# Window attention with a feed-forward block: the first batch's mask added by TensorE instead of VectorE

## The chip, the cores and the metric

One core of one Trainium2 chip runs the whole program. The metric is the device microseconds of an execution; runs are told by their median. The kernel before takes 974.76 us (median of 3 runs, 974.61 to 975.1).

The engines are named as the profile does: PE is TensorE's matmul, PEld its weight load, DVE VectorE, ACT ScalarE, POOL GpSimd, SP SyncE, which issues most of the DMAs here.

## The reference, cut to what matters

There are 8 batches of 8 heads, 512 local and 32 global rows in a head, 64 columns. A local row sees the 32 global keys and the local keys at most 32 places away. The attention's output, all heads of a row side by side, goes through a feed-forward block of 512 to 2048 to 512 columns.

```python
s_g = scale * np.matmul(q_g, k_all.transpose(0, 1, 3, 2))
out_g = np.matmul(sm(s_g), v_all)
s_ll = scale * np.matmul(q_l, k_l.transpose(0, 1, 3, 2))
mask = np.abs(pos[:, None] - pos[None, :]) <= window          # window = 32
s_ll = np.where(mask, s_ll, -1000000000.0)
s_l = np.concatenate([scale * np.matmul(q_l, k_g.transpose(0, 1, 3, 2)), s_ll], axis=-1)
out_l = np.matmul(sm(s_l), np.concatenate([v_g, v_l], axis=2))
...
h = x @ w_in
out = (h - np.tanh(h)) @ w_out
```

## The kernel before, in words

**The work and its tiles.** Heads are taken in pairs (class `Pair`), four pairs to a batch. In a pair, the keys and queries of two heads are loaded (`add_load`), turned on PE with an identity matrix `idr` (`add_turn`, L1046) and copied out of PSUM to `first_kw` and `first_q` (L869). A head has four tiles of 128 queries against 224 keys (`KC`). `scores` makes two tiles of both heads in one visit of PE (L1149), into one PSUM bank a head. `add_softmax` then works a head and a visit: `peak` (L1458) takes each tile's scores from PSUM, adds the tile's mask, scales by -0.125, writes the sum to a `prob` or `t` tile in SBUF and keeps the row's minimum in `st`, one instruction and one accumulator read a tile; `exp` (L1465) makes the exponentials in place on ACT, with their row sums. `add_norms` takes the inverse of the sums on DVE (L1221, L1222) and multiplies on POOL (L1228). `transposes` turns the probabilities on PE (L1170), copies bring them to `keys_first` (L869), and `add_product` multiplies them with the values (L1247) and splits the result in a high and a low part, `x_hi` (L869) and `x_lo` (L1258), for the feed-forward block. Global queries have their own path (L1079, L1080, L1084, L1090, L1097, L1117).

**The feed-forward block** of a batch (class `Chunk`) takes all heads of its 512 rows: hidden columns by L1520 (three passes, high and low parts of `x` and of `w_in`), tanh (L1528), difference (L1531) and its two parts, output by L1568. Its first step can't start before the last pair's `x_hi` is there. From then on, the feed-forward steps of one batch run on PE between the attention of the next. The weights arrive as 64-bit numbers and are joined to 32 bits on ACT and DVE (`rebias` L938, `low` L942, `join` L946), a piece at a time, then split in high and low parts (L869 and L952).

**Constants.** POOL writes the identity into `pg` (`identity`, masks.py:197 and :199) and the four bf16 masks (`mask(j)`, L1644 to L1650), DVE casts the identity to `idr` (L1636).

**The order.** Every step is an `Op` with engines, a duration and a due time; `Order.run` plans them on a model of the engines and writes each engine's instructions in the planned order. On the chip each engine works through its list strictly in that order. Due times come from `CFG` (some 100 numbers) plus `NUDGE`, a table from the place of an Op to a shift of its due time; `CHOICE` adds a cost to one engine of an Op that can go to two. Where the plan sees PE idle for 0.9 us or more between 5 and 72 us, it puts in filler matmuls of a mask with itself (`fill`, L1814) whose result nobody reads.

Of the kernel before, what the change touches and what calls it, by code (L numbers as in the profile page):

```python
# [10 lines left out]
BF16 = mybir.dt.bfloat16  # L11
# [5 lines left out]
P = 128  # L17
D = 64
# [186 lines left out]
def kernel(ctx, tc, q_l, k_l, v_l, q_g, k_g, v_g, w_in, w_out, out):  # L205
# [66 lines left out]
    masks = [cp.tile([P, KC], BF16, name=f"mask{j}") for j in range(NT)]  # L272
    stats = [cp.tile([P, 24], F32, name=f"st{j}") for j in range(2)]
# [19 lines left out]
    def bank(shape, j, dt=F32):  # L293
# [6 lines left out]
        elif len(shape) == 4:  # L300
# [7 lines left out]
               last=-56.3309, o_st0=-386.5366, o_st1=962.4127, o_tw0=-1908.8636, o_tw1=121.285, one=0, p0=167.5456, pen=5.1952,  # L308
               penp=47.4685, s_g=0.6459, s_gl=20.2886, s_kq=73.0039, s_p=1.9417, s_tg=0.5596, s_w=0.6068, s_wl=12.2887,
               step=102.1945, step1=21.2806, lag0=117.1894, hs0=56.6249, tol=0.0795, xs=0.0659, xw=9.5452, o_ld0=-439.2206,  # L310
               o_tn0=1501.0446, o_sg0=1021.2062, o_tg0=289.7609, o_s0=616.7985, o_sp0=196.7798, o_t0=745.3086, o_tpp0=876.351,
               o_vl0=1794.6857, o_vl1=734.9051, o_pv0=1974.7926, o_pvp0=642.1916, o_ld1=1133.7362, o_pv1=890.4116,
               o_pvp1=90.6808, o_s1=-787.3947, o_sg1=-1021.8773, o_sp1=285.1529, o_t1=-1317.1873, o_tg1=-727.1647,
               o_tn1=632.8924, o_tpp1=-8.455, ho0=190.6449, o_tg=2149.4869, o_pv=1266.5023, o_pvp=-608.8611, o_s=-973.7784,
               o_sp=-468.8434, o_t=-622.5358, o_tpp=348.926, o_tn=-382.6256, o_ld=423.028, o_lq=846.3999, o_sg=-1214.8469,
               o_st=-26.0002, o_tw=1592.5009, o_vl=-2037.6091, o_gl=-12.6939, a_kw=0.2609, d_kw=1.0519, s_kw=0.0614, wdi=0.6492,
               wdo=21.9692, L_a_g=0.8656, L_a_kg=6.9738, L_a_ph=2.8878, L_a_qs=197.4661, L_a_w=3.3975, L_a_wn=6.4235,
               L_a_xg=4.0116, L_d_g=0.6393, L_d_gl=0.5557, L_d_kg=0.1783, L_d_kq=1.1326, L_d_ph=1.8089, L_d_pl=8.7171,
               L_d_qh=0.7611, L_d_qs=907.9411, L_d_tg=8.6488, L_d_tp=8.6984, L_d_w=0.4061, L_d_wl=7.1153, L_d_wn=0.8306,
               L_d_xg=0.6352, L_d_y=0.615, L_ho=452.3556, L_hs=43.2601, L_lag=0.3314, L_last=0.1662, L_pen=0.2526, L_penp=1.0537,  # L320
               L_s_g=0.443, L_s_gl=4.8181, L_s_kq=0.3525, L_s_p=0.5472, L_s_tg=0.3595, L_s_w=1.024, L_s_wl=6.2232,
# [686 lines left out]
    class Pair:  # L1008
# [28 lines left out]
        def add_turn(self):  # L1037
# [18 lines left out]
            def queries(e, _):  # L1056
                copy(e, q, box[1])
# [573 lines left out]
    def add_constants():  # L1631
# [3 lines left out]
        def rounded(e, _):  # L1635
            nc.vector.tensor_copy(idr, pg[:, :P])  # L1636
# [214 lines left out]
```

## Time and profile before

| | |
|---|---|
| median of 3 runs | 974.76 us (974.61 to 975.1) |
| the profiled execution | 975.52 us, its span 973.7 us |
| PE busy in the span | 960.3 us (99%), 6453 matmul records |
| DVE, ACT, POOL busy | 580.3 us (60%), 452.1 us (46%), 387.3 us (40%) |
| the chain that ended last | PE 93%, DVE 2%, ACT 2%, SP 1%, DMA 1% |
| filler matmuls (L1814) | 93 |

Busy time of PE includes fillers, and matmuls that wait in its pipe. The chain names for each stretch the engine that the next step waited for, so the few per cent that aren't PE's show where PE itself is not the limit. A line in the rows below is that of kernel.py; L869 is the helper `copy`, used for many tiles. A record of an fp32 matmul comes twice in the trace, so a visit of `scores` with its four products shows as x8.

### The profile page before, as it was taken

What the parts mean: (1) busy time and instruction counts of PE and PEld (TensorE: products, weight loads), DVE (VectorE), ACT (ScalarE), POOL (GpSimd) and SP (SyncE); (2) the same over time, 40 slices, a digit from 0 to 9 for tenths busy, and PEclk for the clock granted to TensorE, in tenths of its full rate; (3) what the DMA queues carried; (4) which work ended last, traced back from release to release, by engine and by line L of the source; (5) the groups of instructions that cost most, each with busy time, mean ns of one, the idle gap of its engine ahead of it and who ended that gap; (6) DMA issues with size and microseconds to landing.
All of it is one profiled execution on the core that took longest, in us unless ns stands there. A gap on an engine that the chain in (4) does not pass through costs nothing.

```text
span 973.7 us, 18494 instructions
## 1 busy us (share of the span) xinstructions
PE 960.3 (99%) x6453; PEld 784.5 (81%) x6453; DVE 580.3 (60%) x1907; ACT 452.1 (46%) x1275; POOL 387.3 (40%) x526
## 2 busy tenths in 40 slices
PE   8899999999999999999999999999999999999998
PEld 5677877888888888888888888888888888888897
DVE  6997667766657555766676567657636544422211
ACT  6966575745455434654355444534535434111111
POOL 4666756534444433434234444333332332211221
PEclk9999999999999999999999999999999999999999
DMA  8565244321223121322123122221202200100010
GB/s 233 151 178 165 84 114 114 92 38 35 50 39 82 33 39 34 88 40 34 32 38 83 23 39 39 71 50 34 50 14 69 39 17 1 44 1 1 1 44 22
DMA packets 195166, 57.32 MB, mean 59 GB/s; under 512 B 179712, under 2 KB 188416, under 8 KB 195072
## 3 DMA queue, kind: packets, MB, share of 16 engines
q1 hardware_dynamic: 193728, 55.61, 24.1%
q8 instruction: 51, 0.84, 0.4%
q10 hardware_dynamic: 1344, 0.52, 0.2%
q14 instruction: 43, 0.35, 0.1%
HBM read 47.19 MB, written 8.91 MB: 58 GB/s over the span
## 4 chain that ended last, share of the span: by engine, by line
PE 93%; DVE 2%; ACT 2%; SPq 1%; issue 1%; DMA 1%; POOL 0%; POOLq 0%; DVEq 0%; ACTq 0%
PE bank L1520 39%; PE bank L1568 38%; PE bank L1247 6%; PE bank L1149 4%; PE bank L1170 4%; PE bank L1339 1%; SPq L1030 0%; PE bank L1046 0%; DMA wraw<-in_q_g_dram 0%; ACT t L1465 0%; ACT pg L1090 0%; POOL prob L1228 0%; DVE keys_first L869 0%; ACT prob L1465 0%; ACT keys_first L869 0%
## 5 line engine op out<-in xcount | busy, mean ns | idle before, releaser
L1537 POOL TENSOR_TENSOR glo<-t,ghi 128x512 fp32r<-128x512 f32 x107 | 139.1, 1301 | 328.9 <-PE bank L1568 130.0
L1528 ACT ACTIVATE t<-bank 128x512 f32<-128x512 f32 x136 | 81.3, 598 | 302.7 <-PE bank L1520 292.3
L1531 DVE TENSOR_TENSOR t<-bank,t 128x512 f32<-128x512 f32 x136 | 93.9, 691 | 202.5 <-ACT t L1528 201.8
L1228 POOL TENSOR_SCALAR prob<-prob,st 128x224 f32<-128x224 f32 x240 | 108.0, 468 | 143.3 <-DVE st L1222 124.9
L1568 PE MATMUL bank<-w_out_hi,ghi 128*128 128x512 f32 x544 | 152.7, 394 | 0.0
L1568 PE MATMUL bank<-w_out_hi,glo 128*128 128x512 f32 x544 | 151.5, 392 | 0.0
L1568 PE MATMUL bank<-w_out_lo,ghi 128*128 128x512 f32 x544 | 151.3, 392 | 0.0
L1520 PE MATMUL bank<-x_hi,w_in_hi 128*128 128x512 f32 x512 | 140.3, 397 | 0.3 <-DVE x_hi L869 0.3
L1520 PE MATMUL bank<-x_lo,w_in_hi 128*128 128x512 f32 x512 | 137.4, 390 | 0.0
L1520 PE MATMUL bank<-x_hi,w_in_lo 128*128 128x512 f32 x512 | 136.2, 390 | 0.0
L1465 ACT ACTIVATE prob<-prob,st 128x224 f32<-128x224 f32 x240 | 113.2, 475 | 14.9 <-DVE st L1458 13.7
L1458 DVE CUSTOM_DVE_ANT_0 prob<-bank,mask 128x224 f32<-128x224 f32 x240 | 80.8, 386 | 64.7 <-PE bank L1149 57.8
L1568 PEld LDWEIGHTS bank<-w_out_lo,ghi 128*128 128x128 f32 x544 | 101.1, 188 | 22.1 <-issue 1.0
L1568 PEld LDWEIGHTS bank<-w_out_hi,glo 128*128 128x128 f32 x544 | 101.0, 188 | 21.9 <-issue 0.7
L1568 PEld LDWEIGHTS bank<-w_out_hi,ghi 128*128 128x128 f32 x544 | 100.2, 188 | 22.2 <-issue 1.4
L1520 PEld LDWEIGHTS bank<-x_hi,w_in_hi 128*128 128x128 f32 x512 | 93.7, 188 | 24.7 <-issue 3.2
L1520 PEld LDWEIGHTS bank<-x_lo,w_in_hi 128*128 128x128 f32 x512 | 95.9, 188 | 20.2
L1520 PEld LDWEIGHTS bank<-x_hi,w_in_lo 128*128 128x128 f32 x512 | 95.7, 188 | 19.7
L869 ACT COPY keys_first<-bank 128x512 f32<-128x512 f32 (+2 forms) x150 | 69.9, 516 | 89.2 <-PE bank L1170 88.3
L1247 PE MATMUL bank<-keys_first,values 128*64 128x160 f32 (+3 forms) x1024 | 68.7, 276 | 2.2 <-DVE keys_first L869 1.1
L1247 PEld LDWEIGHTS bank<-keys_first,values 96*64 96x64 f32 (+1 forms) x1024 | 56.3, 136 | 9.5 <-ACT keys_first L869 2.9
L1381 DVE STREAM_TRANSPOSE gt<-pg 32x128 f32<-32x128 f32 x192 | 53.1, 276 | 10.2 <-POOL pg L1360 4.3
(164 smaller groups left out, 1222.9 us busy)
## 6 DMA issues: line engine op xcount, KB each, us to landing
values<-in_v_l_dram SPq DMA_DIRECT2D x128, 72.0 KB, 2.2
out_dram<-wpair SPq DMA_DIRECT2D x32, 256.0 KB, 2.0
rawkq<-in_k_l_dram SPq DMA_DIRECT2D x96, 64.0 KB, 2.3
rawkq<-in_q_l_dram SPq DMA_DIRECT2D x96, 64.0 KB, 2.2
values<-in_v_g_dram SPq DMA_DIRECT2D x64, 48.0 KB, 2.0
first_q<-in_moe_w_in_dram SPq DMA_DIRECT2D x6, 512.0 KB, 4.5
stage<-in_moe_w_out_dram SPq DMA_DIRECT2D x6, 512.0 KB, 4.0
stage<-in_moe_w_in_dram SPq DMA_DIRECT2D x6, 512.0 KB, 4.0
```

What stands on the lines that cost most here:

```text
L869: (nc.scalar.copy if e == "A" else nc.vector.tensor_copy)(dst, src)
L1149: nc.tensor.matmul(x[:, i, :KC], q, k, start=n == 0, stop=n == len(passes) - 1)
L1228: nc.gpsimd.tensor_scalar(x, x, st[:, c:c + 1], 1.0, op0=ALU.mult, op1=ALU.mult)
L1247: nc.tensor.matmul(box["o"][h.e:h.e + D, o0:o0 + c1 - c0], values[:k, h.two, t + t // 2 + a], keys_first[:k, h.two, pair, a, c0:c1], start ...
L1381: nc.vector.transpose(gt[r, :c], view(src, [(P, c), (1, 32)], 32 * q))
L1458: nc.vector.tensor_tensor_reduce(out=self.pt(2 * tp + i)[:, :KC], in0=getattr(self, f"s_{tp}")[:, i, :KC], in1=masks[2 * tp + i], scale=-0 ...
L1465: nc.scalar.activation(x, x, AF.Exp, bias=col[:, c0 + i:c0 + i + 1], scale=-1.0, accum_out=col[:, 8 + tp + c0 + i:9 + tp + c0 + i])
L1520: nc.tensor.matmul(self.h[s][:, j * n:(j + 1) * n], w[:, cc, f * P:(f + 1) * P], self.x()[xi][:, cc, :n], start=part == 0 and cc == 0 and ...
L1528: nc.scalar.activation(tt_[q], self.h[s], AF.Tanh)
L1531: nc.vector.tensor_sub(tt_[q], self.h.pop(s), tt_[q])
L1537: eng[e].tensor_sub(gg[q][1], tt_[q], f32(gg[q][0]))
L1568: nc.tensor.matmul(self.acc[tt], g[:, j * self.n + tt * P:j * self.n + (tt + 1) * P], low_out(f) if wi else high_out(f), start=s == 0 and ...
```

## The change

In the first batch alone (`self.b == 0`): queries are scaled by -0.125 when they are copied out of PSUM; a matmul of the mask with a diagonal of -0.125 (`diag`, bf16, made by DVE) starts each tile's PSUM sum, and the score matmul adds to it; `peak` becomes one `tensor_reduce` over the two tiles of a visit, which reads PSUM and writes only the minima; `exp` reads the scores from PSUM and writes the probabilities to SBUF. The bank is free after `exp`, before it was after `peak`. The durations that the plan assumes follow (a visit of `scores` 1.25 for 0.85, `peak` 0.62 for 0.94, `exp` 1.25 for 1.31). `CFG` has other numbers, and `NUDGE` and `CHOICE` are other tables; `NUDGE` now starts at Op 0, before it started at 214. All 7 of the other batches keep `peak` and `exp` as they were.

```diff
+    diag = cp.tile([P, P], BF16, name="diag")
...
-    NUDGE = {214: 0.47, 215: 39.97, 216: 57.05, 217: 55.56, 218: -51.2, 219: -791.25, 220: -863.76, 221: -648.08,
+    NUDGE = {0: -7899.31, 1: -10.73, 2: -7743.31, 3: -1965.74, 4: -3399.06, 5: -5069.77, 6: -3511.66, 7: -10838.26,
...
             def queries(e, _):
-                copy(e, q, box[1])
+                if self.b:
+                    copy(e, q, box[1])
+                elif e == "A":
+                    nc.scalar.mul(q, box[1], -0.125)
+                else:
+                    nc.vector.tensor_scalar(q, box[1], -0.125, None, op0=ALU.mult)
...
                 for i in range(2):
+                    for x in () if self.b else t_:
+                        nc.tensor.matmul(x[:, i, :KC], diag, masks[2 * tp + i], start=True, stop=False)
...
-                            nc.tensor.matmul(x[:, i, :KC], q, k, start=n == 0, stop=n == len(passes) - 1)
+                            nc.tensor.matmul(x[:, i, :KC], q, k, start=n == 0 and self.b > 0, stop=n == len(passes) - 1)
...
             def peak(e, _):
+                if not self.b:
+                    nc.vector.tensor_reduce(out=col[:, c0:c0 + 2], in_=getattr(self, f"s_{tp}")[:, :, :KC], op=ALU.min,
+                                            axis=mybir.AxisListType.X)
+                    return
...
-                    nc.scalar.activation(x, x, AF.Exp, bias=col[:, c0 + i:c0 + i + 1], scale=-1.0,
+                    nc.scalar.activation(x, x if self.b else getattr(self, f"s_{tp}")[:, i, :KC], AF.Exp, bias=col[:, c0 + i:c0 + i + 1], scale=-1.0,
...
             def rounded(e, _):
                 nc.vector.tensor_copy(idr, pg[:, :P])
+                nc.vector.tensor_scalar(diag, pg[:, :P], -0.125, None, op0=ALU.mult)
```

What the new numbers do to the order shows in the built programs. On POOL, at the program's start, the list before begins, after four small constants, with the identity (`pg`), and the masks follow:

```order
masks.py:197 MEMSET pg 128x128
masks.py:199 ISA
masks.py:199 AFFINE_SELECT pg<-pg 128x128
L1644 MEMSET mask_89 128x224
L1648 AFFINE_SELECT mask_89<-mask_89 128x96
L1650 AFFINE_SELECT mask_89<-mask_89 128x96 x2
```

In the changed program the same place begins with the masks (L1718 to L1724 there), and the identity is the last of the constants, just ahead of the first probabilities' normalisation (L1293):

```order
L1718 MEMSET mask_92 128x224
L1722 ISA
L1722 AFFINE_SELECT mask_92<-mask_92 128x192
L1724 AFFINE_SELECT mask_92<-mask_92 128x192
L1718 MEMSET mask_89 128x224
```

```order
L1724 AFFINE_SELECT mask_91<-mask_91 128x96
masks.py:197 MEMSET pg 128x128
masks.py:199 AFFINE_SELECT pg<-pg 128x128
L1293 TENSOR_SCALAR prob_97<-prob_97,st_94 128x224 x2
L1293 TENSOR_SCALAR t_68<-t_68,st_94 128x224 x2
```

So the identity moved from the head of POOL's list to behind all four masks.

On PE, at the program's start, the list before has the turns of keys and queries (L1046, and L992 for the global rows), six fillers, and the first scores; these are its first rows:

```order
L1046 MATMUL bank_100<-idr,first_raw 128x128 x4
L1046 MATMUL bank_101<-idr,first_raw 128x128 x4
L992 MATMUL bank_102<-idr,wraw_67 128x64 x4
L1814 LDWEIGHTS mask_90
L1814 MATMUL bank_103<-mask_90 128x224
```

In the changed program the second pair's keys are turned there too, there are no fillers, and the mask matmuls (L1205) come ahead of the first scores (L1213):

```order
L1103 MATMUL bank_101<-idr,first_raw 128x128 x4
L1049 MATMUL bank_102<-idr,wraw_67 128x64 x4
L1103 MATMUL bank_103<-idr,first_raw 128x128 x4
L1103 MATMUL bank_104<-idr,first_raw 128x128 x4
L1205 LDWEIGHTS diag
L1205 MATMUL bank_105<-mask_89,diag 128x224
L1205 LDWEIGHTS diag
L1205 MATMUL bank_106<-mask_89,diag 128x224
L1213 MATMUL bank_105<-first_kw,first_q 128x224
```

Every one of these still reads `idr`, directly or through `first_kw` and `first_q`. Up to its first feed-forward matmul, PE's list has the same products in both programs (36 score matmuls, 128 turns of probabilities, 64 products with values and so on), with 32 mask matmuls more and 86 fillers for 93. Behind it, 8 feed-forward matmuls come ahead of the next batch's first turn of probabilities before, 20 in the changed list.

On DVE, just ahead of the last pair's `x_hi` in the first batch, the list before has:

```order
L946 SCALAR_TENSOR_TENSOR wpair<-wpair 128x512
L942 TENSOR_SCALAR first_q<-first_q 128x512
L946 SCALAR_TENSOR_TENSOR first_q<-first_q 128x512
L869 CAST w_out_hi<-wpair 128x512
L1221 TENSOR_SCALAR st_93<-st_93 128x5
L1222 RECIPROCAL st_93<-st_93 128x4
L869 CAST x_hi_87<-bank_100 128x256
L1258 TENSOR_TENSOR x_lo_88<-bank_100,x_hi_87 128x256
```

In the changed program (L1003 is `join`, L1527 the next batch's `peak`, L1323 `x_lo`):

```order
L1527 ISA prob_98,st_94<-bank_103,mask_90 128x224
L1527 ISA st_94 128x1
L1003 SCALAR_TENSOR_TENSOR first_q<-first_q 128x512
L926 CAST x_hi_87<-bank_108 128x256
L1003 SCALAR_TENSOR_TENSOR stage<-stage 128x512
L926 CAST x_hi_87<-bank_107 128x256
L1323 TENSOR_TENSOR x_lo_88<-bank_108,x_hi_87 128x256
```

The joins of weights still stand there, one of them now between the two parts of `x_hi`. Between DVE's first softmax minimum and the last `x_lo` of the first batch the list has, against before: 16 `tensor_reduce` for 32 of `peak`'s instructions; 3 copies to `keys_first` for 6; one pair's copies to `first_kw` and one of its global columns more; one cast to `x_hi` more; two pieces of weights (`low` and `join`) more. ACT has those copies the other way round, and two `rebias` more.

## Rows read from the trace of the kernel before

**Rows 1.** The profile's page: busy time of each engine, its share of the span, and its instructions.
```profile
PE 960.3 (99%) x6453; PEld 784.5 (81%) x6453; DVE 580.3 (60%) x1907; ACT 452.1 (46%) x1275; POOL 387.3 (40%) x526
```
**Rows 2.** Busy time of each engine by stretch of the span (us from its start).
```profile
core 0: us, PE busy (x) PEld busy (x) DVE busy (x) ACT busy (x) POOL busy (x), PEclk, DMA share, GB/s
10.00:58.53 48.53, 43.73 (x491) 32.85 (x488) 44.98 (x171) 42.56 (x140) 29.21 (x45) 1.00 0.66 180
58.53:62.64 4.11, 3.23 (x28) 2.05 (x25) 3.72 (x10) 1.93 (x7) 4.11 (x6) 1.00 1.01 284
62.64:900.00 837.36, 836.97 (x5514) 683.06 (x5514) 513.97 (x1681) 394.59 (x1105) 332.49 (x444) 1.00 0.23 52
```
**Rows 3.** The chain that ended last, in order of time (start, us, what): three pieces from the first 63 us.
```profile
31.46 0.93 ACT t L1465 x4
57.90 0.34 DVE w_out_hi L869
59.60 2.60 POOL prob L1228 x4
```
**Rows 4.** POOL in order of time, the constants (start, us, what): the identity's two instructions, the first mask's first, the last mask's last.
```profile
0.73 0.20 POOL masks.py:197 MEMSET pg<- 128x128 f32 x1 [0.29 <-POOLq L1833]
1.01 0.29 POOL masks.py:199 TENSOR_SCALAR_AFFINE_SELECT pg<-pg 128x128 f32<-128x128 f32 x1
1.25 0.28 POOL L1644 MEMSET mask<- 128x224 bf16 x1
...
5.63 0.34 POOL L1650 TENSOR_SCALAR_AFFINE_SELECT mask<-mask 128x192 bf16<-128x192 bf16 x1
```
**Rows 5.** PE in order of time, its start, and the same turns some us later.
```profile
3.63 2.02 PE L1046 MATMUL bank<-idr,first_raw 128*128 128x128 f32 x8 [3.63 <-DMA first_raw<-in_k_l_dram]
...
6.20 1.30 PE L1814 MATMUL bank<-mask 128*128 128x224 bf16 x6
7.43 3.35 PE L1149 MATMUL bank<-first_kw,first_q 64*128 64x224 f32 x16
...
13.07 1.97 PE L1046 MATMUL bank<-idr,first_raw 128*128 128x128 f32 x16
```
**Rows 6.** DVE in order of time: the cast of the identity, and three of the first softmax minima (the second and third of those shown follow each other without a gap).
```profile
1.34 0.27 DVE L1636 CAST idr<-pg 128x128 fp32r<-128x128 f32 x1
...
9.46 0.39 DVE L1458 CUSTOM_DVE_ANT_0 t<-bank,mask 128x224 f32<-128x224 f32 x1 [2.50 <-PE bank L1149]
...
10.09 0.39 DVE L1458 CUSTOM_DVE_ANT_0 prob<-bank,mask 128x224 f32<-128x224 f32 x1
...
10.40 0.39 DVE L1458 CUSTOM_DVE_ANT_0 prob<-bank,mask 128x224 f32<-128x224 f32 x1
```
**Rows 7.** DVE in order of time: copies, casts and weights whose number changes; a step's share of DVE is from its start to the next one's.
```profile
13.52 0.20 DVE L869 COPY first_kw<-first_g 128x128 f32<-128x128 f32 x1
...
15.47 1.52 DVE L869 COPY first_kw<-bank 128x192 f32<-128x192 f32 x4
16.92 0.67 DVE L869 COPY first_q<-bank 128x512 f32<-128x512 f32 x1
...
24.26 1.27 DVE L869 COPY keys_first<-bank 128x512 f32<-128x512 f32 x2
25.45 0.96 DVE L1221 TENSOR_SCALAR st<-st 128x5 f32<-128x5 f32 x1
...
49.99 0.42 DVE L869 CAST x_hi<-bank 128x256 fp32r<-128x256 f32 x1
50.32 0.42 DVE L942 TENSOR_SCALAR stage<-stage 128x512 int32<-128x512 int32 x1
50.78 0.74 DVE L946 SCALAR_TENSOR_TENSOR stage<-stage 128x512 int32<-128x512 int32 x1
51.44 0.41 DVE L942 TENSOR_SCALAR stage<-stage 128x512 int32<-128x512 int32 x1
```
**Rows 8.** ACT's groups in the first 66 us, by form (count, busy us, mean ns of one): exponentials from SBUF, a weight's `rebias` from SBUF, a tanh from PSUM.
```profile
L1465 ACT ACTIVATE prob<-prob,st 128x224 f32<-128x224 f32 x20 | 9.4, 476 | 0.0
L938 ACT ACTIVATE stage<-stage 128x512 f32<-128x512 f32 x6 | 4.1, 683 | 1.7 <-DMA stage<-in_moe_w_in_dram 1.7
L1528 ACT ACTIVATE t<-bank 128x512 f32<-128x512 f32 x1 | 0.6, 597 | 0.1
```
**Rows 9.** PE in order of time: fillers.
```profile
44.56 2.57 PE L1814 MATMUL bank<-mask 128*128 128x224 bf16 x25
```
**Rows 10.** PE in order of time: the last product of the first batch, the first feed-forward matmuls, and the two waits among them.
```profile
55.32 1.10 PE L1247 MATMUL bank<-keys_first,values 128*64 128x160 f32 x16 [0.70 <-ACT keys_first L869]
...
58.53 0.94 PE L1520 MATMUL bank<-x_hi,w_in_hi 128*128 128x512 f32 x3
59.78 0.50 PE L1520 MATMUL bank<-x_hi,w_in_hi 128*128 128x512 f32 x1 [0.31 <-DVE x_hi L869]
...
62.24 0.40 PE L1170 MATMUL bank<-idr,prob 64*128 64x64 f32 x6 [0.57 <-POOL prob L1228]
```
**Rows 11.** DVE in order of time: what stands ahead of the last pair's `x_hi`, and the last `x_lo`.
```profile
54.68 0.97 DVE L946 SCALAR_TENSOR_TENSOR wpair<-wpair 128x512 int32<-128x512 int32 x1
...
58.44 0.39 DVE L869 CAST x_hi<-bank 128x256 fp32r<-128x256 f32 x1
...
59.76 0.42 DVE L1258 TENSOR_TENSOR x_lo<-bank,x_hi 128x256 fp32r<-128x256 f32 x1
```

More of the change, by code (lines that the diff above doesn't have):

```diff
@@ L307 @@
                d_w=0.6526, d_wl=0.2437, d_wn=2.573, d_xg=1.1595, d_y=0.4051, gfirst=0, ho=250.6691, hs=53.597, lag=-1.2752,
-               last=-56.3309, o_st0=-386.5366, o_st1=962.4127, o_tw0=-1908.8636, o_tw1=121.285, one=0, p0=167.5456, pen=5.1952,
+               last=-56.3309, o_st0=-977.9826, o_st1=962.4127, o_tw0=-2112.5799, o_tw1=121.285, one=0, p0=167.5456, pen=5.1952,
                penp=47.4685, s_g=0.6459, s_gl=20.2886, s_kq=73.0039, s_p=1.9417, s_tg=0.5596, s_w=0.6068, s_wl=12.2887,
-               step=102.1945, step1=21.2806, lag0=117.1894, hs0=56.6249, tol=0.0795, xs=0.0659, xw=9.5452, o_ld0=-439.2206,
@@ new lines @@
+               L_d_qs=0.1593, L_d_tg=3.5969, L_d_tp=9.6782, L_d_w=0.9189, L_d_wl=0.1991, L_d_wn=8.9376, L_d_xg=0.238,
+               L_d_y=0.3975, L_ho=499.4922, L_hs=34.3753, L_lag=0.1556, L_last=1.7574, L_pen=82.007, L_penp=82.3966,
+               L_s_g=0.3256, L_s_gl=0.073, L_s_kq=0.5094, L_s_p=1.0791, L_s_tg=6.0758, L_s_w=0.2284, L_s_wl=0.5529,
+               L_o_tg=2825.31, L_o_pv=2110.2607, L_o_pvp=-908.8877, L_o_s=0.5423, L_o_sp=3.0684, L_o_t=1.1031, L_o_tpp=0.1634,
+               L_o_tn=63.5915, L_o_ld=0.3308, L_o_lq=11.7512, L_o_sg=-1418.022, L_o_st=2.1266, L_o_tw=126.2042, L_o_vl=1.4794,
@@ L1464, in exp @@
                     x = self.pt(2 * tp + i)[:, :KC]
-                    nc.scalar.activation(x, x, AF.Exp, bias=col[:, c0 + i:c0 + i + 1], scale=-1.0,
+                    nc.scalar.activation(x, x if self.b else getattr(self, f"s_{tp}")[:, i, :KC], AF.Exp, bias=col[:, c0 + i:c0 + i + 1], scale=-1.0,
                                          accum_out=col[:, 8 + tp + c0 + i:9 + tp + c0 + i])
             d = self.pair.due(self.C["o_s"] + self.C["o_sp"] * tp + self.C["o_st"] * self.two)
-            add(("D", 0.94), peak, d + 1, r=[s, ("mask", 2 * tp), ("mask", 1)], w=[p, st], free=[(s, 1)])
-            add(("A", 1.31), exp, d + 1.5, r=[st], w=[p], res=[("inv", tp, self.pair.u)], lat=0.06)
+            if self.b:
+                add(("D", 0.94), peak, d + 1, r=[s, ("mask", 2 * tp), ("mask", 1)], w=[p, st], free=[(s, 1)])
+            else:
+                add(("D", 0.62), peak, d + 1, r=[s], w=[st])
+            add(("A", 1.31 if self.b else 1.25), exp, d + 1.5, r=[st] if self.b else [st, s], w=[p], res=[("inv", tp, self.pair.u)],
+                lat=0.06, free=() if self.b else [(s, 1)])
         def add_values(self):
```

27 lines of the change are left out of this document (12 added, 15 removed), and 1110 rows, old and new, of tables (CHOICE, NUDGE).

## The prediction, made before the changed kernel ran

> **What bounds the kernel now.** I read the busy shares first, then the busy time by stretch, then the chain, then the timelines of the first 63 us. PE is busy 99% of the span [rows 1]. By stretch: from 62.64 to 900 us PE is idle for 0.4 us of 837, while DVE and ACT are far from full [rows 2]. There the kernel is bound by PE's work alone, which the change leaves as it is, so whatever the first batch wins or loses before PE is full comes out at the end, one for one. From 10 to 58.53 us it is another kernel: PE is busy 43.73 of 48.53 us with fillers among it, DVE 44.98, ACT 42.56 [rows 2], and the chain runs through ACT, then DVE, then POOL [rows 3]. The number to predict is when the first feed-forward matmul starts; it is 58.53 now [rows 10], and PE's list up to that place holds the same products in both programs.
>
> PE starts late: its first turn is at 3.63, and a DMA is what ended that wait [rows 5]. The identity was long ready: POOL made it by 1.30 [rows 4], DVE cast it from 1.34 to 1.61 [rows 6].
>
> **The change, part by part.**
>
> *The constants, moved.* POOL's masks run from 1.25 to 5.97, 4.72 us [rows 4]. In the changed list they come first: from 0.73, where POOL starts now, to 5.45. The identity, 0.57 us (0.73 to 1.30) [rows 4], then ends at 6.02, DVE's cast (0.27) [rows 6] at about 6.3, and the first turn starts at about 6.4 instead of 3.63: **+2.8 us**, and with PE everything that waits for it, the loads into buffers that PE must have read included. DVE and ACT have next to nothing that doesn't need a turn first, so nothing covers this. Behind the start the way to the first minimum is 5.8 us now (3.63 to 9.46 [rows 5, 6]). The new list has one group of four turns more on it and, between the two halves of the first scores, two masks; six fillers leave it (1.30 us [rows 5]). At the start eight turns take 2.02 us, later sixteen take 1.97 [rows 5]: the first rows of PE are twice as long as the same form a little later, and four turns cost 1.0, two masks 0.4. I take the two sides as equal.
>
> *Minima on DVE.* Thirty-two instructions leave; each holds DVE for 0.31 us, from the start of one to that of the next [rows 6], 9.9 us together, accumulator reads hidden in them. Sixteen `tensor_reduce` over 448 PSUM elements come. The trace has no such instruction. Nearest is the PSUM copy of 512: two hold DVE for 1.19 us (24.26 to 25.45) [rows 7], so 0.52 for 448 of them at the least, and 0.69 if the full length of one copy stands before the next. That gives 8.3 to 11.0, a gain of 1.6 or a loss of 1.1; I take 0.58, between them and nearer the row's spacing, 9.3: **-0.6**. The plan assumed 0.94 before and 0.62 now for two tiles, a gain of 5 us, but what it replaces took 0.62 in the trace already.
>
> [...]
>
> *The rest of DVE's list up to the last `x_lo`.* Three copies to `keys_first` leave at 0.6 (-1.8); one pair's `first_kw` comes, 1.45 us for two pairs (15.47 to 16.92), so +0.7, and its global columns, +0.2; one cast to `x_hi`, +0.3 (49.99 to 50.32); two pieces of weights, 1.12 each (50.32 to 51.44), +2.2 [rows 7]. Together +1.6, and with the minima **+1.0**. DVE works from 9.46 [rows 6] to 59.76 [rows 11] with only 3.5 us idle in 48.5 [rows 2], so I put this on the path. Between the bounds of the reduce it is 0 to +2.7.
>
> *Exponentials on ACT.* 32 of them read PSUM for SBUF. Nearest rows: a tanh of 512 from PSUM takes 597 ns, a `rebias` of 512 from SBUF 683 [rows 8]. So 0 to 0.09 each, 0 to 2.8 us less. ACT also gets two `rebias` (0.68 each [rows 8]) and three copies to `keys_first`, and loses a pair's `first_kw`. I take it as even and off the path, since DVE is fuller; if ACT is what holds the stage, it is a gain, below.
>
> *Masks on PE.* 32 matmuls of the fillers' form, 25 of which take 2.57 us [rows 9]: 0.10 each, 3.3 us, less seven fillers, 0.7. They stand where PE has room: 87 of the fillers stand between 10 and 58.53, some 9 us that nobody reads, and PE is idle for another 4.8 there [rows 2]. Nothing on the path, as long as that stage ends where DVE lets it. With no such cover they would cost the 2.6.
>
> *PSUM banks and the diagonal.* Scores hold their bank until the exponentials are done, up to 1 us longer (two of 476 ns [rows 8]); all eight banks serve the first batch, so I cost it at nothing. `diag` is one more cast of 0.27 us, behind the identity and beside PE's first turns: nothing. Scaling the queries is the same pass over PSUM as the copy: nothing.
>
> *After the first feed-forward matmul.* Now PE waits there 0.31 for `x_hi` and 0.57 for POOL's normalisation of the next batch [rows 10]. The new list has 20 feed-forward matmuls ahead of that turn instead of 8, so I take the second wait away: **-0.6**. Weights are two pieces further, so no new wait for them.
>
> **The sum:** 2.8 + 1.0 - 0.6 = +3.2 on the profiled 975.52: 978.7. The median is 0.76 below the profiled execution, so I forecast **978.0**.
>
> **The rivals.**
>
> *The late start is absorbed.* The chain lies on ACT's exponentials at 31.46 [rows 3]; if ACT holds the stage and they become 2.8 us shorter, that pays for the start. For it: both engines have idle time in the stage [rows 2]. Against it: DVE has little, and its list gets longer. Then +2.8 from the start, -2.8 from ACT, +1.0 from DVE's list and -0.6 behind: +0.4, 975.2; with the low reduce 974.2.
>
> *Faster: the last `x_hi` comes without a queue.* Now the last pair's product is done at 56.42, but its `x_hi` starts at 58.44, because DVE first works through weights and a normalisation from 54.68 on [rows 10, 11]. If in the new order `x_hi` follows its product at once, 2.0 us go there, at this one place; with ACT's 2.8, with DVE's list at its low bound (0) and with the wait behind the first matmul gone, 2.8 + 0 - 2.0 - 2.8 - 0.6 = -2.6: 972.2. It decides if DVE reaches that cast within 0.3 us of its product's end. Against it: the new list has a join ahead of it and another between its two halves.
>
> *Slower still.* The masks find no room on PE. A score visit stands in PE's list where its queries and keys come ready, which is not where the fillers stood; if each of the 32 masks delays the scores that DVE waits for, the 2.6 us add to the forecast: +5.8, 980.6. For it: some of DVE's waits end with a score matmul, 2.50 us before the first minimum [rows 6]. Against it: the mask matmuls need only `diag` and a free bank, so they can run while PE waits for the keys.
>
> **How the numbers follow.** About 0.2%, 1.95 us, is what a measurement of this kernel can tell from no change. The forecast with the reduce between its bounds (976.9 to 979.7) gets 0.52 and lies beyond 1.95 slower; slower still gets 0.11; absorbed 0.25, within 1.95; faster 0.12. So faster 0.12, same 0.25, slower 0.63. For 8 in 10 the range takes the forecast's own range, the absorbed case down to 974.2, 0.3 below that if the wait for `x_hi` goes too and 0.3 for the spread of the runs, and the slower case: 973.6 to 980.8. What is left out is the faster case and whatever is slower than the slower one.
>
> **What would show it.** The first turn on PE at about 6.4, with DVE's cast of the identity as what ended the wait; the first minimum at about 12.3; `tensor_reduce` holding DVE 0.52 to 0.69; the first feed-forward matmul at 61 to 63; from there to 900 PE idle for well under 1 us. The forecast is wrong if the first feed-forward matmul starts before 60, or if PE waits behind it.

## The result and the profile after

The changed kernel takes **980.12 us** (median of 6 runs, 979.46 to 980.85) where the kernel before took 974.74 beside it (6 runs, 974.45 to 975.64). The ratio is 1.0055 (95% interval 1.0042 to 1.0067), so +5.4 us. The forecast was 978.0 with a range of 973.6 to 980.8: the direction was right and the time lies in the range, but the loss is 5.4 where 3.2 was forecast, and the masks on PE and the held banks, which I had priced at nothing, are where the experiments find the missing part.

Below, a difference in us is a ratio times 975 us; all ratios are to the kernel before, run on the same chip.

First the busy times of the page, which answer to [rows 1]; then the busy time by stretch, which answers to [rows 2]. The stretches are cut at the first feed-forward matmul, which starts at 64.67 now.

```profile
PE 963.1 (98%) x6478; PEld 782.4 (80%) x6478; DVE 560.9 (57%) x1834; ACT 465.8 (48%) x1308; POOL 377.7 (39%) x519
```
```profile
core 0: us, PE busy (x) PEld busy (x) DVE busy (x) ACT busy (x) POOL busy (x), PEclk, DMA share, GB/s
10.00:64.67 54.67, 49.62 (x528) 33.95 (x527) 47.09 (x132) 44.39 (x147) 32.68 (x46) 1.00 0.70 186
64.67:900.00 835.33, 835.27 (x5519) 680.16 (x5517) 496.36 (x1658) 407.68 (x1138) 323.45 (x440) 1.00 0.23 53
```

DVE is idle for 7.6 us between 10 us and the first feed-forward matmul, where it was idle for 3.5 before. It didn't become the fuller engine that my sum had made of it. Behind 64.67 PE is idle for 0.06 us up to 900, so the loss is all in the first batch.

The first feed-forward matmul starts 6.1 us later (64.67 for 58.53 in [rows 10]). From there to the end of the span it is 913.6 us (978.3 less 64.67), 1.5 less than before (973.7 less 58.53). The spans of the two profiled executions differ by 6.1 - 1.5 = 4.6, their times by 4.6 (980.12 for 975.52).

Now the start. POOL's last mask and the identity, DVE's cast, PE's first rows, each in order of time (start, us, what, and in brackets the idle time ahead and what ended it); compare [rows 4 to 6].

```profile
5.23 0.27 POOL L1724 TENSOR_SCALAR_AFFINE_SELECT mask<-mask 128x96 bf16<-128x96 bf16 x1
5.44 0.20 POOL masks.py:197 MEMSET pg<- 128x128 f32 x1
5.71 0.29 POOL masks.py:199 TENSOR_SCALAR_AFFINE_SELECT pg<-pg 128x128 f32<-128x128 f32 x1
```
```profile
6.04 0.23 DVE L1709 CAST idr<-pg 128x128 fp32r<-128x128 f32 x1 [4.30 <-POOL pg masks.py:199]
...
11.69 1.16 DVE L1523 TENSOR_REDUCE st<-bank 128x2 f32<-128x448 f32 x2 [3.07 <-PE bank L1213]
12.76 0.42 DVE L999 TENSOR_SCALAR first_q<-first_q 128x512 int32<-128x512 int32 x1
```
```profile
6.32 1.12 PE L1103 MATMUL bank<-idr,first_raw 128*128 128x128 f32 x4 [6.32 <-DMA values<-in_v_l_dram]
...
12.72 0.36 PE L1205 MATMUL bank<-mask,diag 128*128 128x224 bf16 x2
13.02 0.65 PE L1213 MATMUL bank<-first_kw,first_q 64*128 64x224 f32 x4
13.60 0.36 PE L1205 MATMUL bank<-mask,diag 128*128 128x224 bf16 x2
13.89 0.65 PE L1213 MATMUL bank<-first_kw,first_q 64*128 64x224 f32 x4
14.47 0.66 PE L1103 MATMUL bank<-idr,first_raw 128*128 128x128 f32 x4
```

The first turn starts at 6.32, 2.7 later, and the cast of the identity waited for POOL. (The row on PE names a DMA as the last releaser, a load of `values`, which this turn doesn't read; three of these, issued from 3.87 on, took 2.0 to 2.5 us from issue to landing. The cast at 6.04 is the last thing that a turn needs.) The first minimum starts 2.2 later (11.69 for 9.46). Two reductions hold DVE from 11.69 to 12.76: 0.535 us each.

The rows from 12.72 to 14.47 are one visit of `scores` with its masks: mask pair 0.30, two products of both heads 0.58, and both again, 1.75 in all. Uncut, the same eight records of scores take 0.96 from their start to the next row (17.59 to 18.55 in a run below). So masks cost 0.8 a visit, 0.2 a mask, twice the fillers' 0.10 of [rows 9]: a mask pair takes 0.30 for 0.20, and the visit's scores, cut in two by the second pair, take 1.16 for 0.96.

Next, DVE's waits for scores of the first batch (engine, line, releaser: us in total, times, longest wait), of before from 6 to 62 us and then of after from 6 to 64.7. L1458 is the old minimum, L1523 the new one, L1149 and L1213 are the scores.

```profile
DVE t L1458 <- PE bank L1149: 2.5, 1, 2.5
```
```profile
DVE st L1523 <- PE bank L1213: 4.8, 4, 3.1
```

Before, DVE waited for scores once, ahead of the first minimum. Now it waits four times, 1.7 us of it behind the first minimum: with the scores, PE has become the one that is late. (DVE's wait for turned queries went the other way, 3.3 us before and 0.3 after.) That is the reading on which the experiments were built.

### The profile page after: what moved, and what is told of

The parts are those of the page before. It is cut to its first block, busy times and chain, and to the rows that moved or that the text cites. A ratio compares the mean times of both kernels' runs of the same rounds, so it can differ in the third digit from the quotient of the medians.

```text
span 978.3 us, 18488 instructions
## 1 busy us (share of the span) xinstructions
PE 963.1 (98%) x6478; PEld 782.4 (80%) x6478; DVE 560.9 (57%) x1834; ACT 465.8 (48%) x1308; POOL 377.7 (39%) x519
## 3 DMA queue, kind: packets, MB, share of 16 engines
HBM read 47.19 MB, written 8.91 MB: 57 GB/s over the span
## 4 chain that ended last, share of the span: by engine, by line
PE 95%; DMA 2%; DVE 1%; SPq 1%; POOL 1%; issue 0%; ACT 0%; DVEq 0%; POOLq 0%; ACTq 0%
PE bank L1641 39%; PE bank L1593 39%; PE bank L1312 6%; PE bank L1213 5%; PE bank L1235 4%; PE bank L1404 1%; PE bank L1103 1%; DMA rawkq<-in_k_l_dram 1%; SPq L1087 0%; DMA stage<-in_moe_w_out_dram 0%; POOL prob L1293 0%; DVE st L1523 0%; DMA values<-in_v_g_dram 0%; DVE stage L999 0%; PE bank L1888 0%
## 5 line engine op out<-in xcount | busy, mean ns | idle before, releaser
L1610 POOL TENSOR_TENSOR glo<-t,ghi 128x512 fp32r<-128x512 f32 x105 | 136.1, 1297 | 274.7 <-PE bank L1641 136.2
L1293 POOL TENSOR_SCALAR prob<-prob,st 128x224 f32<-128x224 f32 x240 | 109.5, 474 | 172.1 <-DVE st L1287 124.7
L926 ACT COPY keys_first<-bank 128x512 f32<-128x512 f32 (+2 forms) x154 | 73.0, 516 | 85.6 <-PE bank L1235 82.0
L1534 ACT ACTIVATE prob<-prob,st 128x224 f32<-128x224 f32 x224 | 105.8, 476 | 14.5 <-DVE st L1527 13.2
L1527 DVE CUSTOM_DVE_ANT_0 prob<-bank,mask 128x224 f32<-128x224 f32 x224 | 75.7, 386 | 58.4 <-PE bank L1213 54.3
L1312 PE MATMUL bank<-keys_first,values 128*64 128x160 f32 (+3 forms) x1024 | 66.5, 275 | 0.9 <-ACT t L1534 0.7
```

The source lines that it names most:

```text
L926: (nc.scalar.copy if e == "A" else nc.vector.tensor_copy)(dst, src)
L1293: nc.gpsimd.tensor_scalar(x, x, st[:, c:c + 1], 1.0, op0=ALU.mult, op1=ALU.mult)
L1312: nc.tensor.matmul(box["o"][h.e:h.e + D, o0:o0 + c1 - c0], values[:k, h.two, t + t // 2 + a], keys_first[:k, h.two, pair, a, c0:c1], start ...
L1527: nc.vector.tensor_tensor_reduce(out=self.pt(2 * tp + i)[:, :KC], in0=getattr(self, f"s_{tp}")[:, i, :KC], in1=masks[2 * tp + i], scale=-0 ...
L1534: nc.scalar.activation(x, x if self.b else getattr(self, f"s_{tp}")[:, i, :KC], AF.Exp, bias=col[:, c0 + i:c0 + i + 1], scale=-1.0, accum_ ...
L1610: eng[e].tensor_sub(gg[q][1], tt_[q], f32(gg[q][0]))
```

## The experiments

Two theories stood at the start: that the computation itself costs on PE and by its banks (my theory by then), and that the new order does (rival). For each kernel the table has the ratio with its interval, and where the first feed-forward matmul starts in its profile. A profile is of one execution, which need not be near the median: for the old order with the first two visits the old way it took 979.93 us (median 978.18), for the exponentials earlier on ACT 978.19 (median 979.77). PE's slow start also differs between the traces, by up to 1.5 us (last section). So a microsecond in the last column isn't always the edit's.

| kernel | ratio | us | first feed-forward matmul |
|---|---|---|---|
| before, identity late | 1.0012 (1.0002 to 1.0022) | +1.2 | 59.52 |
| before's computation, the new numbers | 1.0251 (1.0236 to 1.0266) | +24.5 | 74.81 |
| masks on PE alone, two matmuls a head | 1.0066 (1.0054 to 1.0079) | +6.4 | 63.72 |
| masks on PE alone, one matmul a head | 1.0030 (1.0020 to 1.0040) | +2.9 | 61.22 |
| reduction and held banks alone, no mask | 1.0021 (1.0012 to 1.0031) | +2.0 | 61.25 |
| the same, exponentials earlier on ACT | 1.0043 (1.0030 to 1.0057) | +4.2 | 62.06 |
| new computation, old order | 1.0039 (1.0024 to 1.0054) | +3.8 | 63.91 |
| the same, one mask matmul a head | 1.0026 (1.0016 to 1.0035) | +2.5 | 61.51 |
| the same, first two visits the old way | 1.0031 (1.0019 to 1.0043) | +3.0 | 64.82 |
| the change, identity first | 1.0024 (1.0015 to 1.0034) | +2.3 | 61.95 |
| the same, one mask matmul a head | 1.0013 (1.0004 to 1.0022) | +1.3 | 60.86 |
| the same, first two visits the old way | 1.0018 (1.0009 to 1.0027) | +1.8 | 62.47 |
| the change | 1.0055 (1.0042 to 1.0067) | +5.4 | 64.67 |

### The late identity

In the changed kernel, the identity goes back to the head of POOL's list:

```diff
-        out.sort(key=lambda v: (v[0], v[1]))
+        out.sort(key=lambda v: (v[1] != 1, v[0], v[1]))
```

> The changed kernel with one thing undone: the identity stands first in GpSimd's list again, ahead of the masks; every other list is the changed one. Theory (the late identity is paid in full at the end): the first turn falls from 6.32 to about 3.6 us, the first feed-forward matmul from 64.7 to about 62.2, the time from 980.1 to 977.5 (977.0 to 978.2). Rival (the stage waits for loads and for its later order, which hide the start): the first turn is early, the first feed-forward matmul still at 64 to 65, the time 979.5 to 980.3.

Measured: 977.78 us (10 runs), in the theory's range. The first feed-forward matmul stands at 61.95, 2.7 earlier, and the ratio falls from 1.0055 to 1.0024, some 3 us. The term of +2.8 was right.

In the kernel before, the identity and its cast are put behind the masks, and nothing else is moved:

```diff
+        late = [v for v in out if v[1] in (1, 2)]
+        out = [v for v in out if v[1] not in (1, 2)]
+        k = max(i for i, v in enumerate(out) if v[1] in (5, 6, 7)) + 1
+        out[k:k] = late
```

> The kernel before with one thing done: the identity comes behind the masks in GpSimd's list. Theory (the late start is paid in full): the first turn at about 6.3, the time 977.4, 976.9 to 978.0. Rival (the stage has slack that takes some of it up): 974.7 to 976.2.

Measured: 976.63, +1.2, between the two ranges, and the first feed-forward matmul 1.0 later (59.52), although its first turn starts 2.7 later (6.29 for 3.63). So the kernel before takes up more than half of a late start; the changed kernel takes up nothing. PE's rows show where: the first sixteen records of scores start 2.6 later (10.04 for 7.43 [rows 5]), but the next row follows 2.41 us on (12.45) where it followed 3.28 on (10.71), the row behind them is 0.3 shorter (0.48 for 0.74), and a wait of 0.55 us for a load is gone, so the turns that stood at 13.07 [rows 5] start at 13.95, 0.9 later. The larger part is thus PE's slow start (last section), which ended sooner after the first turn in this trace, and the smaller a wait that the kernel had anyway. A late start has no price of its own: it costs what the stage behind it can't give back.

### Order against computation

The changed kernel's `CFG`, `NUDGE` and `CHOICE` with the computation of before:

```diff
-    NUDGE = {214: 0.47, 215: 39.97, 216: 57.05, 217: 55.56, 218: -51.2, 219: -791.25, 220: -863.76, 221: -648.08,
...
+    NUDGE = {0: -7899.31, 1: -10.73, 2: -7743.31, 3: -1965.74, 4: -3399.06, 5: -5069.77, 6: -3511.66, 7: -10838.26,
...
```

> The old computation (VectorE adds the mask, no mask matmuls) planned with the new numbers (the tables of the order): GpSimd's constants and most of SyncE's loads come in the new order, identity last. Theory (the order costs, the computation does not): about 980, 978.5 to 981.5. Rival (the computation costs: mask matmuls and banks that are held until the exponentials): 974 to 977.5, the start's 2.7 at most.

Measured: 1000.17, which neither theory had. The numbers were made for other durations, PE waits all over the stage (0.84 granted clock in 30 to 40 us, 0.66 in 40 to 50), and the run tells only that such tables can't be judged on another computation.

The other half, the new computation with every step where the old order had it (five steps of exponentials had to move ahead of the step that takes their bank):

```diff
+        for o, s in self.exps:
...
+            bad = [place[x[1]] for x in taken[j] if at < place[x[1]] < place[o.seq]]
+            if bad:
+                v = out.pop(place[o.seq])
+                out.insert(min(bad), v)
```

> The new computation in the order of before: every engine's list as before, with mask matmuls ahead of the scores in the same visit, one tensor_reduce for two of VectorE's minima and exponentials from PSUM; five exponential steps move ahead of the step that takes their bank. Theory (the computation is about free): 974.7, 973.5 to 975.7, the first feed-forward matmul at 57.5 to 59.5. Rival (the computation costs 2 us or more): 976.7 to 979.5, the first feed-forward matmul at 60.5 or later, with score matmuls as what VectorE waits for.

Measured: 979.49 (+3.8), so the computation costs without the new order, and the new order is worth some 1.5 us to it once its identity is early (1.0039 to 1.0024; the intervals overlap, so this is not clear of noise). The waits of DVE and PE from 6 to 64 us:

```profile
DVE st L1480 <- PE bank L1170: 8.9, 7, 3.5
...
PE bank L1162 <- ACT t L1491: 1.3, 1, 1.3
PE bank L1162 <- DVE st L1103: 1.1, 1, 1.1
```

DVE waits seven times for scores (L1170), 8.9 us in all, and PE twice for a bank that somebody still reads (L1162 is the mask matmul). That named two suspects, the masks' turn on PE and the held banks.

### Masks on PE, by themselves

The kernel before, with the mask matmuls ahead of the scores; `peak` stays as it was, but adds a mask of zeros, so that the bank is free when it was before:

```diff
+                    for x in () if self.b else t_:
+                        nc.tensor.matmul(x[:, i, :KC], diag, masks[2 * tp + i], start=True, stop=False)
...
-                                                   in1=masks[2 * tp + i], scale=-0.125, scalar=1e30, op0=ALU.add,
+                                                   in1=masks[2 * tp + i] if self.b else nomask, scale=-0.125, scalar=1e30, op0=ALU.add,
```

> The kernel before, with the mask matmuls on TensorE in the first batch's score visits, and the old two VectorE operations per bank, which now add a mask of zeros; banks come free after VectorE as before. One memset of 128 x 224 is added to VectorE's list at the start. Theory A (mask matmuls on the chain): 8 visits by 0.8 us are 6.4, less fillers and waits that they can lie in (0.5 to 2.5 us): 978.5 to 981, first FFN matmul at 62.5 to 65. Theory B (banks): VectorE's list bounds the stage and the masks lie beside it: 974.5 to 976, first FFN matmul at 58.5 to 59.5.

Measured: 981.69, +6.4, a little over the range: eight visits by 0.8 us, as if nothing hid any of it. Of this, 5.2 stands at the first feed-forward matmul (63.72 for 58.53). Behind it PE waits 0.82 for `x_hi` where it waited 0.31 [rows 10]. All 93 fillers are still in PE's list here.

Then with one matmul of 448 columns a head and visit in place of two of 224. The columns are the same, but the visit isn't cut:

```diff
-                    for x in () if self.b else t_:
-                        nc.tensor.matmul(x[:, i, :KC], diag, masks[2 * tp + i], start=True, stop=False)
+                for x in () if self.b else t_:
+                    nc.tensor.matmul(x[:, :, :KC], diag, mask4[:, 2 * tp:2 * tp + 2], start=True, stop=True)
```

> The kernel before with the mask added on TensorE, by one matmul of 448 columns per head and visit, and the old two VectorE operations per bank with a mask of zeros. With two matmuls of 224 the same change gave 981.7 us (+6.2), and a visit of 1.75 us for 0.96; with one of 448 a visit took 1.44 in the run with the new reduction. Theory A (the masks' turn on TensorE is the loss, and the new reduction with its held banks gives some of it back): 8 visits by 0.48 are 3.8, so 978.5 to 980, at or over the 978.1 that the same masks gave with the new reduction. Theory B (masks mostly lie in TensorE's idle time, and the held banks are the loss): 975.5 to 977.

Measured: 978.41, +2.9, 0.1 under the first theory's range. PE in order of time: the second half of a visit with two a head, then a whole visit with one a head, each with the row behind it.

```profile
11.32 0.36 PE L1145 MATMUL bank<-mask,diag 128*128 128x224 bf16 x2
11.62 0.65 PE L1153 MATMUL bank<-first_kw,first_q 64*128 64x224 f32 x4
12.20 0.65 PE L1081 MATMUL bank<-first_kw,first_m 128*64 128x256 f32 x2
```
```profile
17.12 0.54 PE L1145 MATMUL bank<-mask,diag 128*128 128x448 bf16 x2
17.59 1.03 PE L1154 MATMUL bank<-first_kw,first_q 64*128 64x224 f32 x8
18.55 0.65 PE L1082 MATMUL bank<-first_kw,first_m 128*64 128x256 f32 x2
```

From row to row, half a visit takes 0.88 (11.32 to 12.20) with two a head, and a whole one 1.43 (17.12 to 18.55) with one: 0.33 less a visit, 2.6 for eight, and the ratios differ by 3.5 us. Masks cost 8 x 0.8 = 6.4 and 8 x 0.47 = 3.8 by the rows, 6.4 and 2.9 by the ratios, whose intervals are far apart. This is the clearest result of the study: with the fillers left in the list, most of the masks' time on PE went into the end, and 40% of it or more was the cutting and the second matmul a head, not the columns.

The same edit in the kernels with the whole new computation:

> The new computation in the old order, with one mask matmul of 448 columns per head and visit in place of two of 224, both before the visit's scores. The columns are the same, two matmuls and two turns between bf16 and fp32 are fewer. Theory A by columns (masks cost what their 896 columns take, about 0.4 us, and the rest of the 0.8 is the turns between bf16 and fp32): a visit shorter by 0.1 to 0.3 us, eight of them 0.8 to 2.4, so 977 to 978.7. Theory B (banks): 979 to 979.7, as in the run with two per head.

> The changed kernel with the identity first in GpSimd's list (977.8 us) and one mask matmul of 448 columns per head and visit in place of two of 224. Theory A (the masks' turn on TensorE): 0.8 to 2.4 us less, 975.4 to 977. Theory B (banks, or VectorE): 977.5 to 978.

Measured: 978.09 in the old order (+2.5, 1.3 less than with two) and 976.82 with the new order and the identity first (+1.3, 1.0 less). Both times lie in the first theory's range, though in each pair the intervals of the two ratios overlap. The second is the best version with the new computation, and it is still behind the kernel before.

### The reduction and the banks, by themselves

The new computation in the old order without the mask matmuls:

```diff
-                    for x in () if self.b else t_:
-                        nc.tensor.matmul(x[:, i, :KC], diag, masks[2 * tp + i], start=True, stop=False)
...
-                            nc.tensor.matmul(x[:, i, :KC], q, k, start=n == 0 and self.b > 0, stop=n == len(passes) - 1)
+                            nc.tensor.matmul(x[:, i, :KC], q, k, start=n == 0, stop=n == len(passes) - 1)
```

> The new computation in the old order (979.5 us, 3.7 over the kernel before) without its mask matmuls: the first batch's mask is left out, one reduction still takes the minimum of two tiles, and a bank is still held until both exponentials have read it. Theory A, TensorE's mask matmuls: a visit of scores with its four masks took about 1.8 us in the trace of after where a visit without them took 0.96, and TensorE's turn lies on the chain, so with them gone the 3.7 us go and some of the reductions' gain shows: 973.5 to 975.5, first FFN matmul at 57.5 to 59. Theory B, the banks: what costs is the chain reduction, two exponentials, next visit in that bank; it stays, and the time stays at 978 to 979.5, first FFN matmul at 62.5 to 64.

Measured: 977.82, +2.0, where the masks' theory wanted a gain and the banks' theory at least 978. ACT, then PE, in order of time, and the stretches around them:

```profile
19.14 0.69 ACT L952 ACTIVATE wpair<-wpair 128x512 f32<-128x512 f32 x1 [1.04 <-DMA wpair<-in_moe_w_out_dram]
19.73 0.42 ACT L1489 ACTIVATE t<-bank,st 128x224 f32<-128x224 f32 x1
```
```profile
19.50 0.41 PE L1190 MATMUL bank<-idr,t 64*128 64x64 f32 x6
20.73 0.64 PE L1168 MATMUL bank<-first_kw,first_q 64*128 64x224 f32 x2 [0.82 <-ACT t L1489]
21.59 1.35 PE L1168 MATMUL bank<-first_kw,first_q 64*128 64x224 f32 x6 [0.22 <-ACT prob L1489]
```
```profile
20.00:22.00 2.00, 1.05 (x6) 0.71 (x7) 1.63 (x6) 2.00 (x12) 0.00 (x0) 1.00 0.71 173
22.00:24.00 2.00, 2.00 (x10) 1.06 (x8) 1.02 (x2) 1.57 (x5) 1.74 (x4) 0.54 1.05 247
24.00:26.00 2.00, 2.00 (x18) 1.36 (x16) 1.90 (x6) 2.00 (x10) 1.22 (x2) 0.61 0.26 58
```

ACT waits 1.04 us for a load of weights and rebiases them (0.69), and only then comes to the exponentials; PE waits for the bank that they read (0.82 and 0.22); and after that pause the granted clock (the third number from the right) is 0.54 and 0.61 of full speed in the next two stretches. Two records of L1098 hold PE for 0.91 us there (22.87 to 23.78), where two of the same form held it for 0.48 at 1.00 (17.71 to 18.19). From the two clocks I estimate that the fall costs 2 x 0.46 + 2 x 0.39 = 1.7 us of PE's full speed. That is most of the +2.0, and not of this execution alone: the mean granted clock of all nine is 0.997 or 0.998, while it is 0.999 or 1.000 in all but one of the 23 of the kernel before beside them. The changed kernel has such a pause without the fall: PE is busy for 0.83 of the 2 us from 24 to 26 there, and the clock stays at 1.00 in that stretch and in the next ones.

So the held bank could be the cause, or only ACT's list and the clock behind it. I moved each pair of exponentials right behind its reduction on ACT, ahead of the weights (`m` is the reduction's step):

```diff
+        for o, m in self.exps:
+            place = {v[1]: i for i, v in enumerate(out)}
+            if place[o.seq] > place[m.seq] + 1:
+                v = out.pop(place[o.seq])
+                out.insert(place[m.seq] + 1, v)
```

> The run without mask matmuls (977.8 us; the first batch's mask is left out here too), with each head's two exponentials placed in ScalarE's list right behind the reduction that they wait for, ahead of the FFN weights' copies that stood in between. In the run before, TensorE waited 0.8 us at 20.7 for a bank whose exponentials stood behind a copy of weights (19.14 to 19.81), stood still for about 1 us, and its granted clock was 0.54 and 0.61 in 22 to 26 us. Theory A (the held banks cost by ScalarE's list, and by the fall of the clock that the stall brings): no such stall, clock 1.00 throughout, 973.5 to 975.7, first FFN matmul at 57.5 to 59. Theory B (a bank that is held until its exponentials costs wherever they stand): 977 to 978.5, first FFN matmul at 60.5 to 62.

Measured: 979.77, +4.2, over the ranges of both theories (the profiled execution is the fastest of its five, 978.19), and my theory fell. The clock stays at 1.00 in the first batch, but PE's waits for banks are still there, and ACT's other work is later now. PE's longest waits from 6 us on:

```profile
PE bank L1053 <- ACT prob L1482: 1.8, 2, 1.4
PE bank L1129 <- POOL pg L1109: 1.7, 1, 1.7
PE bank L1161 <- ACT t L1482: 1.0, 1, 1.0
PE bank L1091 <- ACT first_kw L876: 1.0, 1, 1.0
PE bank L1161 <- ACT prob L1482: 0.6, 1, 0.6
```

L1053 turns the next keys, L1161 are scores: 3.4 us of PE's waits are for exponentials. In the kernel before, PE's waits in this stage have none for an exponential, and 0.2 for a minimum. Three of the five executions have a mean clock of 1.000 and still lose 2.7 to 4.3 us. So in both placements PE waits for banks that ACT has yet to read, and the loss doesn't need the fall of the clock. That the held bank alone makes it is argued and not shown: ACT's list is another one here, and PE also waits for what comes later from ACT and POOL.

### Back to the old way in the first two visits

PE is at its slowest in the first visit (in the run with the new order and one mask matmul a head its masks and scores hold PE for 2.65 us, 7.30 to 9.95, and those of the second visit for 1.44, 11.08 to 12.52), and DVE has nothing to do yet (it waits 3.9 us for that visit's scores); so the first pair's two visits went back to DVE's masks, with the rest as in the two runs with one mask matmul (`new` then chooses matmul, reduction and the exponentials' source):

```diff
+        def new(self, tp):
+            return self.b == 0 and (self.j, tp) not in [(0, 0), (0, 1)]
...
-                for x in () if self.b else t_:
+                for x in t_ if self.new(tp) else ():
```

> The run with the identity first and one mask matmul per head (976.8 us), but with the first pair's two visits of scores in the old way: no mask matmuls, two VectorE operations per bank. There the masks took 0.88 and 0.48 us on TensorE and VectorE had waited 3.9 us for the first bank. Theory A (masks on the chain): 1.4 us less on TensorE, less 0.3 on VectorE's four operations: 975.3 to 976.2, level with the kernel before. Theory B (VectorE's list bounds): 976.8 to 977.5.

> The old order with one mask matmul per head (978.1 us), with the first pair's two visits of scores in the old way. Theory A: the first two visits give back their masks (0.86 + 0.48 us), which the chain then loses again in part at the transfers that come later (the kernel before waited 0.55 for one there): 976.7 to 977.6. Theory B: 978 to 978.5.

Measured: 977.58 (+1.8, where +0.2 to +1.1 was hoped for, and just over the second theory's range) and 978.18 (+3.0, in the second theory's range). Nothing came of it. In the first of them, PE's wait and the stretches after it:

```profile
14.37 0.43 PE L1050 MATMUL bank<-idr,wraw 64*128 64x64 f32 x4 [2.07 <-DVE st L1533]
```
```profile
12.00:14.00 2.00, 0.30 (x3) 0.07 (x1) 1.73 (x9) 1.88 (x8) 0.00 (x0) 1.00 1.13 308
14.00:16.00 2.00, 1.28 (x13) 1.19 (x13) 1.87 (x13) 1.94 (x8) 1.74 (x4) 1.00 1.04 277
16.00:18.00 2.00, 2.00 (x24) 1.70 (x23) 2.00 (x5) 1.43 (x6) 1.87 (x2) 0.59 0.83 188
18.00:20.00 2.00, 2.00 (x11) 1.18 (x11) 0.45 (x3) 1.72 (x4) 1.57 (x5) 0.55 1.01 262
```

The time won on PE became a wait for DVE's old minima (2.07; in the other run 2.67 for a load), and behind it the clock fell to 0.59 and 0.55, which is 1.7 us again by the same estimate (0.61 and 0.53 in the other run). The fall is not in every execution, though. Of the eleven of the first run, five with a mean clock of 0.999 or 1.000 took 975.62 to 976.46 us, and six with 0.998, the profiled one among them, 977.58 to 978.36. The run that it was made from, with its masks in place, divides in the same way: six took 975.82 to 976.82, five 977.39 to 977.95. The median of the upper-clock executions is 0.9 over the kernel before in both (976.04 for 975.14, 976.42 for 975.52). So the masks of these two visits gave nothing back even where the clock held, and having them there didn't always keep it up.

## Why the prediction was right in direction and short in size

The first turn (6.32 for "about 6.4"), the reduction and PE's idle time up to 900 came as foretold; the first feed-forward matmul did not, 64.67 for 61 to 63. That the time still lies in the range is owed to the "slower still" rival, which set its upper end.

*Late identity, +2.8.* Right: 2.7 at the first feed-forward matmul, some 3 in time. It is half of the loss.

*After the first feed-forward matmul, -0.6.* Right in sign, larger: both waits are gone, and the way from there to the end is 1.5 shorter.

*Minima on DVE, -0.6, and the rest of its list, +1.6.* The reduction takes 0.535 us where I took 0.58, near my lower bound; 16 of them are 1.3 us less than what they replace (9.9 less 8.6). The step that put DVE's list on the path failed, though: DVE has 7.6 us idle in the stage and waits for PE, so neither term could be read off the end.

*Masks on PE, nothing.* This is the step that failed. The price was half of the true one (0.10 a mask from [rows 9], 0.2 in place), since I took it from fillers that follow each other, and these stand between scores. And the cover wasn't there. I counted 9 us of fillers and 4.8 of idle time as room. But only seven fillers leave the list; 86 still run in their places, for 10.0 us (a group from 6 to 66 us: busy us, mean ns), and the last 14 stand right ahead of the first feed-forward matmul. PE, DVE's last cast to `x_hi`, and the group:

```profile
63.39 1.51 PE L1888 MATMUL bank<-mask 128*128 128x224 bf16 x14
64.67 2.09 PE L1593 MATMUL bank<-x_hi,w_in_hi 128*128 128x512 f32 x8
```
```profile
63.32 0.42 DVE L926 CAST x_hi<-bank 128x256 fp32r<-128x256 f32 x1
```
```profile
L1888 PE MATMUL bank<-mask 128*128 128x224 bf16 x86 | 10.0, 260 | 0.0
```

`x_hi` is whole at 63.74, so up to 0.9 us of the loss is PE working through fillers; before, the 18 in that place ended ahead of `x_hi`. And the idle time lies where PE waits for its next operand, while a mask stands in a visit whose keys and queries are ready and whose scores DVE waits for. No run took the fillers out, so how much of the masks' price they could give back isn't known. My rival "slower still" had said that each mask delays the scores, and named 980.6; I gave it 0.11. That its number comes so close is luck: it has half the price of a mask, and a longer way on DVE that didn't come.

*PSUM banks, nothing.* Failed too. Without masks, the reduction and the held banks together still lose 2.0 to 4.2 us; the traces show PE waiting for exponentials there, and in the run with 2.0 the fall of the clock behind such a wait.

*What the parts give together.* Masks alone +6.4, reduction with held banks +2.0 or more, and both +3.8 in the same order: they don't add up. With two mask matmuls a head, the reduction gives back some 2.6 (1.0066 to 1.0039, the intervals touch); with one, 0.4 (1.0030 to 1.0026, the intervals overlap). The new order gives back some 1.5 (not clear of noise), and then its identity takes 3. In the run without masks PE paused and its clock fell, in the profiled execution of the same order with masks it did not; but that is one stretch, and with the exponentials moved the clock held and the loss was larger. So how what the identity leaves of the 5.4 divides between masks and banks stays open. A reduction with a bank that is free again ahead of the exponentials was not tried.

*Exponentials on ACT, even and off the path.* The size is right: from PSUM they take 444 to 447 ns (32 of them, by form), from SBUF 476 [rows 8], 1.0 us for all. They aren't all off the path: the chain of the changed kernel goes through four of them at 39.06 (0.97 us).

```profile
L1534 ACT ACTIVATE prob<-bank,st 128x224 f32<-128x224 f32 x16 | 7.0, 444 | 3.6 <-DVE st L1523 3.6
L1534 ACT ACTIVATE t<-bank,st 128x224 f32<-128x224 f32 x16 | 7.0, 447 | 2.8 <-DVE st L1523 2.0 <-POOL prob L1293 0.6
```

## What to carry to other kernels

Idle time on an engine is room only for work that may run at that moment, and fillers only if they leave the list (here 86 of 93 stayed); for work in front of what the next engine waits for, the cover was nil here, so ask of each added instruction who waits behind it. Price it from rows in which it stands among the same neighbours: here the same matmuls cost twice as much between fp32 products as in a row of their own. And before moving work from one engine to another, see which one waits for the other in the new place: relieving DVE by 1.3 us was paid with 2.9 to 6.4 on PE.

## What the runs showed of the hardware

- One bf16 matmul of 448 columns in place of two of 224, ahead of eight fp32 products and not between them, made a visit 1.43 for 1.75 us.
- Just after PE's start the same instruction takes about twice its later time, though the granted clock is told as 1.00 there: in the run with masks alone, four records of scores held PE for 1.04 us at 7.87 (to 8.91) and for 0.58 at 11.62 (to 12.20). How long this lasts differs from trace to trace: from the start of the first sixteen records of scores to the next row it is 3.28 us in the kernel before (7.43 to 10.71), 2.41 with its identity late (10.04 to 12.45), 2.06 in the run without masks (7.75 to 9.81) and 1.73 in the old order with the first two visits the old way (7.55 to 9.28), the same eight products each time. Traces of two kernels can so differ by 1.5 us ahead of anything that the edit does.
- In three runs (no mask, and the two with the first two visits the old way) a pause in PE's work (0.82, 2.07 and 2.67 us), with other short ones around it, was followed by stretches with a granted clock of 0.53 to 0.61. The run with the new numbers alone had falls too (0.84 in 30 to 40 us, 0.66 in 40 to 50). In the run with early exponentials PE paused for 1.0 of the 2 us from 24 to 26, and the clock stayed at 1.00. So whether a pause costs more than itself can't be told from its length alone here.
